# Whole-sequence loads by head pair, merged constants, a catch-up at the end of the first phase, and FFN units paced until the next block, in a chunk-selecting attention followed by a squared-ReLU FFN

## The chip, the cores and the metric

The kernel runs on one core of one Trainium2 chip. The metric is the device time of one execution in microseconds (us), median of the runs. Before the change it was 330.38 us (three runs, 330.23 to 330.52; with a fourth run, 330.43).

The engines are called as the profile calls them: PE multiplies matrices, PEld loads its weights, DVE is the vector engine, ACT the scalar engine, POOL the general engine (here it issues most loads and masks the diagonal), SP issues the other transfers.

## The reference, cut to what matters

Four batches, eight heads, 768 positions, head dimension 64. For each query, the keys' chunks of 32 are ranked by an upper bound from each chunk's smallest and largest key; only the best six causal chunks are attended. The result goes through an FFN of 512 to 2048 to 512.

```
k_min, k_max = k_chunks.min(axis=3), k_chunks.max(axis=3)
ub = sum(maximum(q * k_min, q * k_max), axis=-1)          # one bound per query and chunk
top_chunks = argsort(where(causal, ub, -1e9))[..., -6:]
scores = where(sel & causal_by_position, q @ k.T / 8, -1e9)
attn = softmax(scores) @ v
x = attn.transpose(0, 2, 1, 3).reshape(3072, 512)
out = square(maximum(x @ w_in, 0)) @ w_out
```

## The kernel before

Work is cut into eight phases: each batch has a first-half phase (queries 0 to 383) and a second-half phase (queries 384 to 767). A phase goes through four head pairs. Three kinds of work are interleaved:

- stage A of a pair ("selection"): transpose keys and queries on PE, copy them out of PSUM, reduce them to chunk bounds, rank, and write the rank's mask rows beside the queries;
- stage B of a pair: scores on PE (`ps`), exponentials on ACT (`e`), values on PE (`av`), then Ln, Ln and Exp on ACT for the reciprocal (`rc`), and two products on DVE into `xT`;
- FFN units of the block that was finished last: 16 "up" units (4 matmuls `ph`, a ReLU, a square) and 12 "down" units (4 matmuls `py` each), 28 for each block of 384 tokens. They are put between score matmuls to fill PE while ACT makes exponentials. `run_ffn` is called after each score matmul and decides how many.

```
def run_ffn(cols):                       # before
    pace["due"] += cols * pace["rate"]
    while pace["due"] >= 1.0 and ffn:
        ffn.pop(0)[1]()
        pace["due"] -= 1.0
# ... cut ...
    behind.append(lambda j=j, es=es: values(j, es))     # values lag behind scores
    if len(behind) == HT + LAG:                          # HT = 3, LAG = 2
        for _ in range(HT):
            behind.pop(0)()
# ... cut: for each phase ph ...
    cols = sum(768 if x[2] == 0 else 1920 for x in items if x[0] == "B")
    pace["rate"] = (len(ffn) + nunits - KEEP) / cols if ph else 0.0    # nunits 28, KEEP 8
```

The rate counts the units that are left plus the 28 that the lagging values will release early in the phase, less 8 that are kept for the next phase's start.

The build puts the instructions of each engine into a list order of its own; an instruction with nothing to wait for can come long before its place in the program (the memsets of L410 in the next section, written for the second phase, run from 5.27 us).

The softmax here doesn't subtract the row's maximum and nothing guards it: scores larger than these inputs give would overflow.

## Time and profile before

330.38 us; the profiled run spans 328.7 us. The head of the page: the span, the busy time of each engine with its share, and the busy share of PE, DVE and the granted PE clock in 40 slices of 8.2 us (a digit is tenths).

```profile
span 328.7 us, 6090 instructions
PE 294.6 (90%) x2076; PEld 158.7 (48%) x2096; DVE 219.1 (67%) x678; ACT 218.2 (66%) x540; POOL 99.1 (30%) x237
PE   1397699999998999999999999999999999999995
DVE  7987879778899867999485488994576213421420
PEclk9999999999999999999999999999999999999999
```

PE looks full from the sixth slice on. It is not: matmuls overlap (at 54 us a 384-column matmul has a row of 0.33 us, and the next starts 0.162 us after it), so a "busy" PE has room, and the first slices run at half speed although the clock row shows nines. The timeline of PE shows it (start, length, line, what, idle time before with its releaser):

```profile
37.63 0.82 PE L345 MATMUL av_646<-e,vo 128*128 128x384 bf16 x3 [1.77 <-DVE xT L369]
41.61 0.80 PE L288 MATMUL ph<-xT,w_in_sb 128*128 128x384 bf16 x2 [1.58 <-DVE xT L369]
43.26 1.81 PE L288 MATMUL ph<-xT,w_in_sb 128*128 128x384 bf16 x5
54.21 1.88 PE L288 MATMUL ph<-xT,w_in_sb 128*128 128x384 bf16 x10
```

Five FFN matmuls took 1.81 us at 43 us, ten took 1.88 us at 54 us. The pitches show the two speeds: matmuls of 384 columns that follow each other start 0.32 us apart up to 47 us, 0.162 us after 48.

DVE at the start, from its timeline:

```profile
5.27 0.48 DVE L410 MEMSET vo<- 128x512 bf16 x1
5.85 2.11 DVE L410 MEMSET vo<- 128x512 bf16 x4
7.97 0.72 DVE L201 COPY kqc<-kT 64x384 bf16<-64x384 bf16 x2
```

The memsets belong to the second phase in the program, but run first; the first key copy waits for them until 7.97 us.

The end of the chain that ended last (start, length, what):

```profile
296.55 3.88 PE py L302 x18
300.49 2.97 PE py L302 x13
304.13 10.53 PE ph L288 x60
314.93 10.10 PE py L302 x46
325.06 0.59 ACT ob L307
```

### The profile page before, as it was taken

How to read it: one execution, taken by the hardware profiler on the slowest of the kernel's cores; microseconds unless marked ns; L12 is line 12 of the kernel's file. 1: busy time of each engine (PE TensorE's matmuls, PEld its weight loads, DVE VectorE, ACT ScalarE, POOL GpSimd, SP SyncE). 2: the span in 40 equal slices, each digit the busy share in tenths (PEclk: the TensorE clock that was granted, in tenths of full speed). 3: DMA queues.
4: the chain of work that ended last, by engine and by line, in shares of the span. 5: the costliest groups of instructions: out<-in, count | busy, mean ns of one | idle time of the engine just before them, and what ended most of it. 6: DMA issues, size and time to landing. Idle time of an engine off the chain costs nothing.

```text
span 328.7 us, 6090 instructions
## 1 busy us (share of the span) xinstructions
PE 294.6 (90%) x2076; PEld 158.7 (48%) x2096; DVE 219.1 (67%) x678; ACT 218.2 (66%) x540; POOL 99.1 (30%) x237
## 2 busy tenths in 40 slices
PE   1397699999998999999999999999999999999995
PEld 1143344454454445555455455554555555554542
DVE  7987879778899867999485488994576213421420
ACT  6064556786666559887479766787579679973731
POOL 8886840452410722202142222111122311210000
PEclk9999999999999999999999999999999999999999
DMA  6999999999590891000193010000100000001001
GB/s 45 151 148 195 134 159 210 119 127 98 60 102 3 56 194 40 2 1 3 41 101 52 2 66 32 2 1 3 64 34 0 32 34 32 2 0 64 35 33 64
DMA packets 81371, 20.87 MB, mean 63 GB/s; under 512 B 74836, under 2 KB 77756, under 8 KB 81340
## 3 DMA queue, kind: packets, MB, share of 16 engines
q0 software_dynamic: 77344, 13.63, 53.8%
q1 hardware_dynamic: 3996, 6.85, 5.6%
q8 instruction: 16, 0.26, 0.3%
q14 instruction: 15, 0.12, 0.1%
HBM read 27.26 MB, written 6.29 MB: 102 GB/s over the span
## 4 chain that ended last, share of the span: by engine, by line
PE 55%; DVE 24%; ACT 8%; DMA 6%; issue 3%; POOL 2%; ACTq 0%; DVEq 0%
PE py L302 21%; PE ph L288 13%; PE ps L379 8%; DMA w_out_sb<-in_moe_w_out_dram 6%; DVE kr L206 4%; ACT rc L359 4%; DVE xT L369 3%; DVE qsc L201 3%; ACT e L383 2%; DVE kqc L201 2%; PE sT L249 2%; DVE qsc L254 1%; ACT rc L362 1%; PE kT L194 1%; DVE qp L216 1%
## 5 line engine op out<-in xcount | busy, mean ns | idle before, releaser
L383 ACT ACTIVATE e<-ps 128x384 bf16<-128x384 f32 (+2 forms) x288 | 108.6, 430 | 37.1 <-PE ps L379 34.6
L386 POOL TENSOR_SCALAR_AFFINE_SELECT e<-e 128x128 bf16<-128x128 bf16 x192 | 55.9, 302 | 183.4 <-ACT e L383 181.6
L288 PE MATMUL ph<-xT,w_in_sb 128*128 128x384 bf16 x512 | 105.3, 331 | 4.8 <-ACT ht L293 3.0
L293 ACT ACTIVATE ht<-ph 128x384 bf16<-128x384 f32 x128 | 63.3, 503 | 22.6 <-PE ph L288 17.0
L379 PE MATMUL ps<-qsc,kqc 88*128 88x384 bf16 (+2 forms) x288 | 72.2, 303 | 6.2 <-ACT e L383 2.8
L288 PEld LDWEIGHTS <-w_in_sb 128*128 128x128 bf16 x512 | 48.7, 98 | 38.9 <-issue 13.4
L345 PEld LDWEIGHTS <-vo 128*128 128x128 bf16 x288 | 28.0, 101 | 20.9 <-DVE xT L369 3.2
L379 PEld LDWEIGHTS <-kqc 88*128 88x128 bf16 x288 | 27.2, 100 | 21.9 <-issue 5.7
L307 ACT COPY ob<-py 128x512 f32<-128x512 f32 x24 | 14.2, 590 | 25.7 <-PE py L302 25.5
L206 DVE TENSOR_REDUCE kr<-kT 128x24 bf16<-128x768 bf16 (+1 forms) x40 | 30.3, 793 | 0.3
L201 DVE COPY kqc<-kT 64x768 bf16<-64x768 bf16 (+1 forms) x40 | 18.9, 474 | 16.9 <-PE kT L194 16.3
L254 DVE COPY qsc<-sT 24x640 bf16<-24x640 bf16 (+2 forms) x40 | 16.7, 417 | 7.6 <-PE sT L249 6.8
L201 DVE COPY qsc<-qT 64x768 bf16<-64x768 bf16 (+1 forms) x40 | 18.9, 473 | 1.2 <-PE qT L194 0.6
L194 PE MATMUL kT<-ident,kn 128*64 128x128 bf16 x192 | 11.2, 240 | 8.7 <-POOL ident masks.py:199 4.3
L362 ACT ACTIVATE rc<-rc 128x384 f32<-128x384 f32 x32 | 16.5, 516 | 0.2
L194 PEld LDWEIGHTS <-kn 128*64 128x64 bf16 x192 | 6.8, 116 | 16.3 <-issue 6.5
L194 PE MATMUL qT<-ident,qn 128*64 128x128 bf16 x192 | 11.1, 237 | 1.5 <-DMA qn<-in_q_dram 1.3
L194 PEld LDWEIGHTS <-qn 128*64 128x64 bf16 x192 | 6.7, 114 | 9.6 <-DVE kr L206 4.3
L249 PE MATMUL sT<-ident,selb 128*128 128x128 bf16 x80 | 8.6, 233 | 2.7 <-DVE selb L241 2.4
L229 PE MATMUL ub<-kbd,qp 128*128 128x48 bf16 x80 | 7.7, 190 | 3.4 <-DVE qm L217 2.1
L211 DVE COPY kbd<-kr 64x48 bf16<-64x48 bf16 (+1 forms) x40 | 10.0, 251 | 0.5
L234 DVE TENSOR_TENSOR ubm<-ub,ubmask 128x240 f32<-128x240 f32 (+2 forms) x20 | 7.1, 353 | 4.5 <-PE ub L231 4.3
(648 smaller groups left out, 483.5 us busy)
## 6 DMA issues: line engine op xcount, KB each, us to landing
out_dram<-ob SPq DMA_DIRECT2D x24, 256.0 KB
kn<-in_k_dram POOLq DMA_DIRECT2D x3, 768.0 KB, 9.5
qn<-in_q_dram POOLq DMA_DIRECT2D x3, 768.0 KB, 11.6
vo<-in_v_dram POOLq DMA_DIRECT2D x3, 768.0 KB, 10.2
w_out_sb<-in_moe_w_out_dram POOLq DMA_DIRECT2D x1, 2048.0 KB, 21.0
w_in_sb<-in_moe_w_in_dram POOLq DMA_DIRECT2D x1, 1536.0 KB, 11.7
vo<-in_v_dram POOLq DMA_DIRECT2D x6, 128.0 KB, 7.3
kqc<-kqc SPq DMA_DIRECT2D x15, 36.0 KB
```

The source lines that it names most:

```text
L194: nc.tensor.matmul(pt[D * hh:D * hh + D, 128 * j:128 * (j + 1)], lhsT=nat[nm, b][:, 2 * hp + hh, n0 * HT + j], rhs=ident, is_transpose=Tru ...
L201: nc.vector.tensor_copy(ops[s][hh][0:D, cols], pt[rows])
L206: nc.vector.tensor_reduce(kr[:, mm], pt.rearrange("d (c j) -> d c j", j=CH), axis=AX.X, op=op)
L254: nc.vector.tensor_copy(qs[s][hh][D:KC, 128 * u0:128 * t1], sT[32 * hh:32 * hh + NC, :])
L288: nc.tensor.matmul(ph, lhsT=w_in_sb[:, ki, 128 * f:128 * (f + 1)], rhs=xT[:, ki], start=(ki == 0), stop=(ki == NKI - 1))
L293: nc.scalar.activation(ht, ph, ACT.Relu)
L302: nc.tensor.matmul(py, lhsT=h2[f][:, 128 * t:128 * (t + 1)], rhs=w_out_sb[:, f, :], start=(f == 0), stop=(f == NFI - 1))
L345: nc.tensor.matmul(hold["av"][hh][:, off:], lhsT=vo[b % 2].rearrange("p h n d -> p (h n d)")[:, c0:c0 + 2 * D], rhs=es[hh][:, off:], start ...
L362: nc.scalar.activation(rc, rc, ACT.Exp, scale=-1.0)
L379: nc.tensor.matmul(ps[:, off:], lhsT=kq[s][hh][:, 128 * j:128 * (j + 1)], rhs=qs[s][hh][:, q0 + off:q1], start=True, stop=True)
L383: nc.scalar.activation(e[:, off:], ps[:, off:], ACT.Exp, scale=scale)
L386: nc.gpsimd.affine_select(out=e[:, off:off + 128], in_=e[:, off:off + 128], compare_op=ALU.is_ge, fill=0.0, base=0, channel_multiplier=-1, ...
```

## The change

Its intent: load keys, queries and values by head pair over the whole sequence, so that stage A of any half can start; do the constants in a few large memsets before the first data come; take work off DVE in the first phase; release the first block's FFN units sooner; and spread the FFN units so that they don't run out while the next block's values are pending. The diff, cut to its core:

```
-    load_qk(0, 0, 2, (0,), "k")          # halves of the sequence, one or six heads at a time
-    load_qk(0, 2, H, (0,))
+    load_qk(0, "k"); load_qk(0, "q"); load_qk(1)      # a head pair, whole sequence, 192 KB each
+    load_v(0); load_qk(2); load_v(1); load_qk(3); load_w_in(0, 4); load_v(2); load_v(3)
# ... batch 1 and later: pair by pair instead of 768 KB at a time (cut) ...

-    def set_constants(s): ...            # five small memsets for each of 8 sets; vo[1] in 6 parts
+    nc.vector.memset(kbds, 0.0)          # one tile for all sets
+    nc.vector.memset(selbs[:, :, NT - 1], 0.0)
+    nc.vector.memset(selbs[:, :, 0:NT - 1, :, NC:], 0.0)
+    nc.vector.memset(vo[1]... .bitcast(F32)[:, :, D // 2:], ONES)    # two bf16 ones per word

+                if nm == "q" and first:                  # first halves of batch 0
+                    nc.scalar.copy(ops[s][hh][0:D, cols], pt[rows])
-                for hh in range(2):
-                    nc.vector.tensor_copy(kbd[s][rows, :, hh, 12 * n0:12 * n1], kr[rows])
+                nc.vector.tensor_mul(kbd[s][:, :, :, 12 * n0:12 * n1], kr..., own...)

-    put(0, NP, ("A", 0, (1,), True))
+    put(0, NP, L(catch_up), ("A", 0, (1,), True))        # catch_up empties "behind"

-    KEEP = 8
+    KEEP = (12, 7)      # kept at the end of a second-half phase, of a first-half phase
     def run_ffn(cols):
-        pace["due"] += cols * pace["rate"]
+        late = left.get(pace["tb"], 0) > 0               # the last block's values still pending
+        n = len(ffn) if late else len(ffn) - pace["keep"]
+        over = pace["until"] if late else pace["cols"]
+        if n > 0:
+            pace["due"] += n * min(1.0, cols / max(over, cols))
+        pace["until"] -= cols; pace["cols"] -= cols
```

More of the change, by code (lines that the diff above doesn't have):

```diff
@@ L43 @@
     NEG = -32768.0
+    ONES = 1.0 + 0x3F80 / 2.0 ** 23
     NP = H // 2
@@ L63, with load_qk @@
     nat = {}
-    def load_qk(b, h0, h1, halves=(0, 1), what="kq"):
+    def load_qk(p, what="kq"):
+        b, h = p // NP, 2 * (p % NP)
         for nm, src in (("k", k), ("q", q)):
@@ L72, in load_qk @@
                                      name=nm + "n")
-            j0, j1 = HT * halves[0], HT * (halves[-1] + 1)
-            if j1 - j0 == NT:
-                nc.gpsimd.dma_start(
-                    out=nat[nm, b][:, h0:h1].rearrange("p h j d -> p (h j) d"),
-                    in_=src[b, h0:h1].rearrange("h (j p) d -> p (h j) d",
-                                                p=128))
-                continue
-            if h1 - h0 <= j1 - j0:
-                for h in range(h0, h1):
-                    nc.gpsimd.dma_start(
-                        out=nat[nm, b][:, h, j0:j1],
-                        in_=src[b, h, 128 * j0:128 * j1].rearrange(
-                            "(j p) d -> p j d", p=128))
-                continue
@@ L87, in load_qk @@
-            for j in range(j0, j1):
-                nc.gpsimd.dma_start(
-                    out=nat[nm, b][:, h0:h1, j],
-                    in_=src[b, h0:h1, 128 * j:128 * (j + 1)].rearrange(
-                        "h p d -> p h d"))
+            nc.gpsimd.dma_start(
+                out=nat[nm, b][:, h:h + 2].rearrange("p h j d -> p (h j) d"),
+                in_=src[b, h:h + 2].rearrange("h (j p) d -> p (h j) d", p=128))
     vo = [consts.tile([128, H, NT, 2 * D], BF16, tag=f"vo{s}", name="vo")
@@ L95 @@
           for s in range(2)]
-    def load_v(b, half=None):
-        if half is None:
-            nc.gpsimd.dma_start(
-                out=vo[b % 2][:, :, :, 0:D].rearrange("p h j d -> p (h j) d"),
-                in_=v[b].rearrange("h (j p) d -> p (h j) d", p=128))
-            return
-        for j in range(HT * half, HT * half + HT):
-            nc.gpsimd.dma_start(
-                out=vo[b % 2][:, :, j, 0:D],
-                in_=v[b, :, 128 * j:128 * (j + 1)].rearrange("h p d -> p h d"))
@@ L109, with load_v @@
-    load_qk(0, 0, 2, (0,), "k")
+    def load_v(p):
+        b, h = p // NP, 2 * (p % NP)
+        nc.gpsimd.dma_start(
+            out=vo[b % 2][:, h:h + 2, :, 0:D].rearrange("p h j d -> p (h j) d"),
+            in_=v[b, h:h + 2].rearrange("h (j p) d -> p (h j) d", p=128))
+    load_qk(0, "k")
     ident = consts.tile([128, 128], BF16, tag="ident")
     make_identity(nc, ident)
-    load_qk(0, 0, 2, (0,), "q")
-    load_qk(0, 2, H, (0,))
+    load_qk(0, "q")
+    load_qk(1)
     NSET = 2 * NP
-    kq, qs, kbd, selb = [], [], [], []
@@ L118 @@
-    for s in range(NSET):
-        kq.append([consts.tile([KC, S], BF16, tag=f"kq{s}{hh}", name="kqc")
-                   for hh in range(2)])
-        qs.append([consts.tile([KC, S], BF16, tag=f"qs{s}{hh}", name="qsc")
-                   for hh in range(2)])
-        kbd.append(consts.tile([128, 2, 2, NC], BF16, tag=f"kbd{s}", name="kbd"))
-        selb.append(consts.tile([128, NT, 2, 32], BF16, tag=f"selb{s}",
-                                name="selb"))
-    def set_constants(s):
-        nc.vector.memset(kbd[s], 0.0)
-        for hh in range(2):
-            nc.vector.memset(qs[s][hh][D:KC, 0:128], 0.0)
-        nc.vector.memset(selb[s][:, :, :, NC:], 0.0)
-        nc.vector.memset(selb[s][:, NT - 1], 0.0)
-        for hh in range(2):
-            if (s, hh) == (0, 0):
-                nc.scalar.activation(
-                    kq[0][0][D:KC, :].rearrange("c (a j) -> c a j", j=CH),
-                    ident[0:NC, 0:NC].unsqueeze(2).to_broadcast([NC, NC, CH]),
-                    ACT.Copy, scale=NEG)
-            else:
-                nc.sync.dma_start(out=kq[s][hh][D:KC, :], in_=kq[0][0][D:KC, :])
@@ L142 @@
-    set_constants(0)
-    set_constants(1)
+    kqs = consts.tile([KC, NSET, 2, S], BF16, tag="kqs", name="kqc")
+    qss = consts.tile([KC, NSET, 2, S], BF16, tag="qss", name="qsc")
+    selbs = consts.tile([128, NSET, NT, 2, 32], BF16, tag="selbs", name="selb")
+    kbds = consts.tile([128, NSET, 2, 2, NC], BF16, tag="kbds", name="kbd")
+    kbd = [kbds[:, s] for s in range(NSET)]
+    kq = [[kqs[:, s, hh] for hh in range(2)] for s in range(NSET)]
+    qs = [[qss[:, s, hh] for hh in range(2)] for s in range(NSET)]
@@ new lines, with kq_rows @@
+    selb = [selbs[:, s] for s in range(NSET)]
+    def kq_rows(i):
+        dst = kqs[D:KC, i // 2, i % 2]
+        if i == 0:
+            nc.scalar.activation(
+                dst.rearrange("c (a j) -> c a j", j=CH),
+                ident[0:NC, 0:NC].unsqueeze(2).to_broadcast([NC, NC, CH]),
+                ACT.Copy, scale=NEG)
+        else:
+            nc.sync.dma_start(out=dst, in_=kqs[D:KC, 0, 0])
+    own = consts.tile([128, 2], BF16, tag="own")
+    nc.vector.memset(own, 0.0)
+    for hh in range(2):
+        nc.vector.memset(own[D * hh:D * hh + D, hh:hh + 1], 1.0)
@@ L144 @@
+    nc.vector.memset(kbds, 0.0)
+    nc.vector.memset(selbs[:, :, NT - 1], 0.0)
+    nc.vector.memset(selbs[:, :, 0:NT - 1, :, NC:], 0.0)
+    for s in range(NSET):
+        nc.vector.memset(qss[D:KC, s, :, 0:128], 0.0)
+    nc.vector.memset(vo[1].rearrange("p h j d -> p (h j) d").bitcast(F32)[
+        :, :, D // 2:], ONES)
+    for i in range(2 * NP):
+        kq_rows(i)
     for j in range(2):
@@ L170, in load_w_in @@
             in_=moe_w_in[:, cols].rearrange("(ki p) f -> p ki f", p=128))
-    load_v(0, 0)
+    load_v(0)
+    load_qk(2)
+    load_v(1)
+    load_qk(3)
     load_w_in(0, 4)
+    load_v(2)
+    load_v(3)
     def load_w_out():
@@ L188, in stage_a @@
         m = QB * n1 - u0
-        pool, tag = (psf, "ff") if p < NP and n1 == 1 else (pst, "tp")
+        first = p < NP and n1 == 1
+        pool, tag = (psf, "ff") if first else (pst, "tp")
         for nm in ("k", "q"):
@@ L200, in stage_a @@
                 rows = slice(D * hh, D * hh + D)
-                nc.vector.tensor_copy(ops[s][hh][0:D, cols], pt[rows])
+                if nm == "q" and first:
+                    nc.scalar.copy(ops[s][hh][0:D, cols], pt[rows])
+                else:
+                    nc.vector.tensor_copy(ops[s][hh][0:D, cols], pt[rows])
             if nm == "k":
@@ L208, in stage_a @@
                         axis=AX.X, op=op)
-                for hh in range(2):
-                    rows = slice(D * hh, D * hh + D)
-                    nc.vector.tensor_copy(
-                        kbd[s][rows, :, hh, 12 * n0:12 * n1], kr[rows])
+                nkc = NC // 2 * nt
+                nc.vector.tensor_mul(
+                    kbd[s][:, :, :, 12 * n0:12 * n1],
+                    kr.unsqueeze(2).to_broadcast([128, 2, 2, nkc]),
+                    own.unsqueeze(1).unsqueeze(3).to_broadcast(
+                        [128, 2, 2, nkc]))
                 yield
@@ L258 @@
     xTs = {}
-    nunits = NFI + (QB // 128) * (NFI // 4)
     behind = []
-    KEEP = 8
+    KEEP = (12, 7)
     LAG = 2
@@ L317, in ffn_units @@
         return units
-    pace = {"due": 0.0, "rate": 0.0}
+    pace = {"due": 0.0}
     def run_ffn(cols):
-        pace["due"] += cols * pace["rate"]
+        late = left.get(pace["tb"], 0) > 0
[3 more added lines that the diff above has]
+            pace["due"] += n * min(1.0, cols / max(over, cols))
+        pace["until"] -= cols
+        pace["cols"] -= cols
         while pace["due"] >= 1.0 and ffn:
@@ L408, in put, with catch_up @@
         phases[ph][i:i] = items
+    def catch_up():
+        while behind:
+            behind.pop(0)()
     L = lambda f, *a: ("L", lambda: f(*a))
@@ L412 @@
         put(0, max(hp - 1, 0), ("A", hp, (0,), True))
-    put(0, 1, L(load_qk, 0, 0, H, (1,)), L(load_w_in, 4, NFI))
-    put(0, 2, L(load_v, 0, 1))
-    put(0, NP, ("A", 0, (1,), True))
+    put(0, 2, L(load_w_in, 4, NFI))
+    put(0, NP, L(catch_up), ("A", 0, (1,), True))
+    put(0, NP, L(load_qk, NP), L(load_qk, NP + 1))
     for hp in range(1, NP):
         put(1, 0, ("A", hp, (1,), False))
-    put(1, 0, L(load_qk, 1, 0, H), L(load_w_out), L(load_v, 1))
+    put(1, 0, L(load_w_out))
     for b in range(1, B):
@@ L424 @@
         put(e + 1, 0, ("A", p0 + NP - 1, (0, 1), False))
-        if b + 1 < B:
-            put(e + 1, 1, L(load_qk, b + 1, 0, H))
-            put(e + 1, NP, L(load_v, b + 1))
-    phases[0][1:1] = [L(set_constants, 2), L(set_constants, 3)]
-    for ss in range(NP, NSET):
-        put(1, 1, L(set_constants, ss))
-    for j in range(NT):
-        put(1, j // 2 + 1, L(nc.vector.memset, vo[1][:, :, j, D:], 1.0))
-    for ph, items in enumerate(phases):
-        cols = sum(768 if x[2] == 0 else 1920 for x in items if x[0] == "B")
-        pace["rate"] = (len(ffn) + nunits - KEEP) / cols if ph else 0.0
+    for hp in range(2, NP):
+        put(1, hp - 1, L(load_qk, NP + hp))
+    for hp in range(NP):
+        put(1, hp, L(load_v, NP + hp))
+        for b in range(2, B):
+            put(NBLK * b - 2, hp, L(load_qk, NP * b + hp))
+            put(NBLK * b - 1, hp, L(load_v, NP * b + hp))
+    for i in range(2 * NP, 2 * NSET):
+        put(1, 1, L(kq_rows, i))
+    for ph, items in enumerate(phases):
+        b, blk = divmod(ph, NBLK)
+        pace["tb"] = ph - 1
+        pace["cols"] = NP * (768 if blk == 0 else 1920)
+        pace["until"] = 1408 if blk == 0 else 1536
+        pace["keep"] = KEEP[(blk + 1) % NBLK]
         for x in items:
@@ L448 @@
             ffn.pop(0)[1]()
-    while behind:
-        behind.pop(0)()
+    catch_up()
     while ffn:
```

## The prediction

> **What bounds the kernel.** The page gives PE 90% of 328.7 us, DVE 67%, ACT 66%, but a busy PE hides losses. I charged each matmul of the timeline its warm pitch: 162 ns for 384 columns, 216 ns for 512. All need about 257 us. The missing 72 us:
>
> - first matmul at 4.3 us; 3.6 us of tail after the last;
> - about 38 us between 4 and 48 us. There the timeline starts 384-column matmuls 0.32 us apart, half speed, though the page's granted clock reads full; from 48 us it is 0.162 us. [...]
> - about 28 us of bubbles after 48 us, densest in batch 1 (90 to 140 us), where DVE is 80 to 95% busy.
>
> The head is a DVE chain: the windows table has DVE 85 to 97% busy from 5 to 30 us. 5 us of memsets come first; then memsets of the second value buffer (0.48 us each) run from 5.3 us, so the first key copy, whose transposes ended at 5.2 us, starts at 7.97 us. A head pair of the first phase costs DVE about 6.4 us. The last pair's values wait 1.8 us for xT and end in xT at 41.6 us; only then do FFN matmuls flow.
>
> **What the change does.**
> - Merged memsets: about 4 us by element counts at the traced rate (1 element per ns), done as the first keys land (about 5 us). First copy near 5.5 us: gain 2 to 2.5 us, on the chain.
> - First-phase query copies (2 x 0.35 us per pair) go to ACT, which has room; two block-diagonal copies (2 x 0.34 us) become one multiply, about 0.2 us by estimate. About 4 us over the phase, on the chain.
> - Last pair's values run at once: 2 to 3 us, on the chain.
> - Loads: same bytes, whole sequence first. By the traced 150 to 165 KB/us the fourth pair lands near 16 us, before DVE gets to it. Half of batch 1's keys and queries now precede w_out, which should land near 50 us against 60.1; first needed near 51 us, so it may cost 1 to 2 us.
> - So xT of block 0 is ready at 32 to 34 us, full pitch comes at 39 to 41 us. Gain in the head 8 to 10 us.
> - Pacing: about 33 FFN units run in a first-half block's phase and 23 in a second-half one, against 28 each. By traced durations the second-half phase had about 37 us of PE work, the first-half about 30; now about 34 each. Units no longer run out while the previous block's last values are pending. Gain 4 to 6 of the 28 us.
>
> **Prediction:** 330.4 - 9 - 5, less for new collisions: 315 us, 307 to 323 in 8 of 10. Faster by over 2%: 0.87; within 2%: 0.11; slower: 0.02.
>
> **What would show it:** first key copy near 5.5 us; last xT of block 0 near 33 us; 0.162 us pitch from about 40 us; w_out landing near 50 us, PE wait on it under 2 us; loss after that about 23 us; tail 3.6 us.
>
> **What would make it wrong:** the list order that the build makes, not program order, decides (set-up meant for later ran first before), so memsets or catch-up may land elsewhere; w_out or later key loads late behind one another in the saturated queue; q copies on ACT delaying exps; 12 kept units turning the second-half phase ACT-bound (about 36 us), so that balance gains nothing.

It gave a rule for when full speed comes, which the traces do not show, and put full speed 6.7 us after 41.6 us; the clock record has it at 47.1 us, 5.5 us after, and 3.9 us after PE's matmuls begin to follow each other almost without gaps (43.26 us). The forecast's step from `xT` at 32 to 34 us to full pitch at 39 to 41 us is about those 6.7 us and was the author's estimate. 330.4 less 9 less 5 is 316.4, put down as 315.

The numbers behind three of its phrases: ACT "has room" since it is busy for 10.26 of the 25 us from 5 to 30 us before the change; the one multiply's 0.2 us was an estimate without a source, and the trace of after has 0.21 us (128x48); the queue is "saturated" as the page of before has DMA at 9 from the second to the tenth slice (8 to 82 us).

## More of the kernel before

In stage A, the part that the change touches:

```
for hh in range(2):
    nc.vector.tensor_copy(ops[s][hh][0:D, cols], pt[rows])     # keys or queries out of PSUM
# ... cut: keys only: max and min over chunks into kr, then
for hh in range(2):
    nc.vector.tensor_copy(kbd[s][rows, :, hh, 12 * n0:12 * n1], kr[rows])
# ... cut: queries only
nc.vector.tensor_scalar_max(qp[:, 0:m], pt[:, u0 - QB * n0:], 0.0)
nc.vector.tensor_scalar_min(qm[:, 0:m], pt[:, u0 - QB * n0:], 0.0)
```

The trace's clock record begins at 47.1 us with full speed; before it there is no record, and the page fills the row with nines.

Busy time by engine in the last four attention phases (a first-half and a second-half phase of batch 2, then of batch 3, counted from 0):

```profile
core 0: us, PE busy (x) PEld busy (x) DVE busy (x) ACT busy (x) POOL busy (x), PEclk, DMA share, GB/s
158.70:188.70 30.00, 29.06 (x199) 16.00 (x200) 17.34 (x48) 21.71 (x57) 9.49 (x25) 1.00 0.48 54
188.70:230.70 42.00, 40.28 (x324) 22.30 (x325) 33.20 (x97) 30.98 (x81) 7.38 (x24) 1.00 0.05 20
230.70:260.70 30.00, 29.06 (x199) 15.99 (x200) 17.35 (x48) 21.71 (x57) 7.29 (x24) 1.00 0.07 27
260.70:295.20 34.50, 33.33 (x203) 18.99 (x204) 10.64 (x25) 29.84 (x79) 6.99 (x24) 1.00 0.06 24
```

In the first three of these phases PE sets the length (PE busy 96 to 97%, ACT 72 to 74%); in the last one, which has no selection work left, ACT is busy for 29.84 of 34.50 us.

## The result, and the profile after

The kernel after took 328.40 us (328.30 to 328.73, 4 runs) beside 330.43 us of the kernel before: ratio 0.9941, interval 0.9924 to 0.9958. A ratio here is the mean time of one kernel's fast runs over that of the other's of the same rounds, so it is not quite the ratio of the medians. By the mark of 2% this is "the same". The prediction of 315 us (307 to 323) was wrong: of 14 us, two came.

The page of after, the lines that answer to those of before:

```profile
span 326.6 us, 6096 instructions
PE 296.2 (91%) x2096; PEld 159.0 (49%) x2096; DVE 209.1 (64%) x619; ACT 220.4 (67%) x548; POOL 109.6 (34%) x254
PE   1587699999988999999999999999999999999995
DVE  6865668888899878996755278995855113340420
PEclk9999999999999999999999999999999999999999
```

DVE lost 10 us of work, as planned, and the time hardly noticed. (20 more matmuls of PE are recorded, not made: some records were missing from the trace of before.)

Where did the time go? I cut both traces at the first exponential of chosen phases, and at the last exponential's end. All values in us, from the starts and ends of the exponentials in the trace; the last column is the span.

```
                          head  phase 1  batch 1  batch 2  batch 3   tail    span
before                   45.48    37.14    76.08    71.97    64.55  33.42   328.7
after                    42.61    36.25    73.28    71.81    66.46  36.19   326.6
after less before        -2.87    -0.89    -2.80    -0.16    +1.91  +2.77    -2.0
new pacing alone (d1)    45.48    37.24    71.72    71.80    66.37  36.18   328.8
d1 less before            0.00    +0.10    -4.36    -0.17    +1.82  +2.76    +0.1
```

"Head" is all until the first exponential of phase 1, "tail" all after the last exponential. Up to 224 us the kernel after had earned 6.7 us; then it gave back 4.7 us, 1.9 in the last batch and 2.8 in the tail. Part of the 6.7 is only work put off: at the start of batch 2 the kernel before has run 77 FFN units and the kernel after 72.75 (weight loads in the trace, four to a unit). Four "down" units take about 3.5 us (an estimate from the tail below: 10.36 us for 12), and they are run in the tail. The run with the new pacing alone (below) has the same two losses, so they are the pacing's.

The tail, in the chain that ended last:

```profile
291.04 10.36 PE py L300 x48
302.08 10.53 PE ph L286 x60
312.61 10.38 PE py L300 x48
323.01 0.59 ACT ob L305
```

Before, 6.9 us of kept "down" matmuls stood here ahead of the last block (3.88 and 2.97 us); now 10.36 us, 48 matmuls, 12 units. They run at full speed (one starts 0.216 us after the other, as in the tail of before) and PE waits for nothing there; they are just late. The predicted tail of 3.6 us is the time after the last matmul, and it stayed (before 328.7 less 325.0, after 326.6 less 323.0); that an extra four units would stand before it was overlooked.

The last four attention phases:

```profile
152.10:186.40 34.30, 33.48 (x221) 17.95 (x219) 17.74 (x47) 22.38 (x57) 7.86 (x24) 1.00 0.15 30
186.40:224.00 37.60, 36.09 (x308) 20.44 (x306) 32.64 (x94) 30.53 (x80) 7.64 (x25) 1.00 0.06 22
224.00:258.20 34.20, 33.38 (x220) 17.90 (x219) 17.72 (x47) 22.28 (x57) 6.82 (x23) 1.00 0.06 24
258.20:290.40 32.20, 30.71 (x191) 17.58 (x189) 10.47 (x25) 29.26 (x79) 7.30 (x25) 1.00 0.07 25
```

The phases were balanced as planned: 30.0 and 42.0 us became 34.3 and 37.6. Their sum did not change (72.0, 71.9), because PE sets the length of both (busy 33.48 of 34.30 us and 36.09 of 37.60): a unit moved costs as much there as it saved here. In the last phase, where ACT is busy 29.26 of 32.20 us, taking five units away (27.25 FFN units before, 22.25 after, counted by their weight loads in the trace, four to a unit) shortened it by only 2.3 us, while the phase before grew by 4.2 us.

The start. DVE, from its timeline:

```profile
3.77 1.34 DVE L128 MEMSET vo<- 128x1536 f32 x1 [0.37 <-issue]
6.01 0.72 DVE L198 COPY kqc<-kT 64x384 bf16<-64x384 bf16 x2 [0.90 <-PE kT L188]
12.66 0.29 DVE L215 TENSOR_SCALAR qp<-qT 128x256 bf16<-128x256 bf16 x1 [0.36 <-ACT qsc L196]
17.20 0.29 DVE L215 TENSOR_SCALAR qp<-qT 128x256 bf16<-128x256 bf16 x1 [0.81 <-ACT qsc L196]
22.12 0.29 DVE L215 TENSOR_SCALAR qp<-qT 128x256 bf16<-128x256 bf16 x1 [0.71 <-ACT qsc L196]
```

The constants are done in time: the second value buffer's ones, six memsets of 512 elements before (0.48 us each), are one of 1536 words now (1.34 us). Back-to-back memsets of 128x512 bf16 start 540.7 ns apart in before, those of 24x128 words 140.6 ns apart in after: 1.04 ns per element by the difference. (Their rows in the trace are 485 and 165 ns long.) The first key copy starts at 6.01 us instead of 7.97; what it waits for now is data (the first keys, 192 KB, land at 5.39 us, 4.07 us after their issue began, 1.14 us of it the issue on POOL; two loads of 48 KB landed at 3.92 and 4.85 us before). But DVE then waits for ACT: `qp` reads the same PSUM tile as ACT's two query copies (0.95 us together), and in this trace it starts only when they are done: three waits of 0.36, 0.81 and 0.71 us. The prediction counted no such wait.

And PE at the end of the first phase:

```profile
31.82 0.80 PE L350 MATMUL av_470<-e,vo 128*128 128x384 bf16 x3 [1.09 <-DVE xT L374]
35.54 0.80 PE L350 MATMUL av_494<-e,vo 128*128 128x384 bf16 x3 [1.06 <-DVE xT L374]
39.50 0.80 PE L286 MATMUL ph<-xT,w_in_sb 128*128 128x384 bf16 x2 [1.64 <-DVE xT L374]
41.98 0.85 PE L384 MATMUL ps<-qsc,kqc 88*128 88x384 bf16 x2
```

The last scores of the first phase are exponentiated by 31.1 us, but the first block's `xT` is ready only at 39.4 us (41.6 before, 32 to 34 predicted): each pair's values wait until the products of the pair before free the one pair of value banks, 3.7 us from the third pair's values to the fourth's. In the same stretch the selection for pair 0's second half runs from 28.7 us (transposes) to 41.7 us (mask rows), and the next scores wait for it. DVE even stood idle for 2.6 us at 27.2 us. Full speed comes at 45.7 us instead of 47.1 (39 to 41 predicted); the clock record begins there, and the page's row shows nines before it, though matmuls of 384 columns start 0.32 us apart at 41 us.

### The profile page after: what moved, and what is told of

Read it like the earlier page. It is cut to its first block, busy times and chain, and to the rows that moved or that the text cites. A ratio compares the mean times of both kernels' runs of the same rounds, so it can differ in the third digit from the quotient of the medians.

```text
span 326.6 us, 6096 instructions
## 1 busy us (share of the span) xinstructions
PE 296.2 (91%) x2096; PEld 159.0 (49%) x2096; DVE 209.1 (64%) x619; ACT 220.4 (67%) x548; POOL 109.6 (34%) x254
## 4 chain that ended last, share of the span: by engine, by line
PE 67%; DVE 13%; ACT 11%; issue 4%; POOL 3%; DMA 2%; ACTq 0%; POOLq 0%
PE py L300 22%; PE ph L286 19%; PE ps L384 10%; ACT e L388 4%; ACT rc L364 4%; DVE xT L374 3%; PE kT L188 2%; DVE qsc L198 2%; DMA kn<-in_k_dram 2%; PE sT L248 2%; ACT ht L291 2%; ACT rc L367 2%; DVE kr L203 1%; PE qT L188 1%; PE ub L228 1%
## 5 line engine op out<-in xcount | busy, mean ns | idle before, releaser
L388 ACT ACTIVATE e<-ps 128x384 bf16<-128x384 f32 (+2 forms) x288 | 110.0, 434 | 28.0 <-PE ps L384 24.9
L286 PE MATMUL ph<-xT,w_in_sb 128*128 128x384 bf16 x512 | 109.9, 332 | 6.0 <-ACT ht L291 4.2
L384 PE MATMUL ps<-qsc,kqc 88*128 88x384 bf16 (+2 forms) x288 | 74.3, 304 | 3.8 <-ACT e L388 3.3
L291 ACT ACTIVATE ht<-ph 128x384 bf16<-128x384 f32 x128 | 64.3, 509 | 13.5 <-PE ph L286 11.3
L198 DVE COPY qsc<-qT 64x768 bf16<-64x768 bf16 (+1 forms) x32 | 16.1, 504 | 3.4 <-PE qT L188 3.0
L85 POOL DMA_DIRECT2D vo<-in_v_dram x16 | 16.4, 1036 | 2.5 <-PE ps L384 1.9
L75 POOL DMA_DIRECT2D kn<-in_k_dram x16 | 16.6, 1039 | 1.5 <-POOLq L480 0.8
L75 POOL DMA_DIRECT2D qn<-in_q_dram x16 | 16.4, 1031 | 0.0
L188 PE MATMUL qT<-ident,qn 128*64 128x128 bf16 x192 | 10.3, 237 | 1.5 <-DMA qn<-in_q_dram 1.1
## 6 DMA issues: line engine op xcount, KB each, us to landing
w_in_sb<-in_moe_w_in_dram POOLq DMA_DIRECT2D x1, 1536.0 KB, 11.2
```

The source lines that it names most:

```text
L75: nc.gpsimd.dma_start(out=nat[nm, b][:, h:h + 2].rearrange("p h j d -> p (h j) d"), in_=src[b, h:h + 2].rearrange("h (j p) d -> p (h j) d" ...
L188: nc.tensor.matmul(pt[D * hh:D * hh + D, 128 * j:128 * (j + 1)], lhsT=nat[nm, b][:, 2 * hp + hh, n0 * HT + j], rhs=ident, is_transpose=Tru ...
L286: nc.tensor.matmul(ph, lhsT=w_in_sb[:, ki, 128 * f:128 * (f + 1)], rhs=xT[:, ki], start=(ki == 0), stop=(ki == NKI - 1))
L291: nc.scalar.activation(ht, ph, ACT.Relu)
L384: nc.tensor.matmul(ps[:, off:], lhsT=kq[s][hh][:, 128 * j:128 * (j + 1)], rhs=qs[s][hh][:, q0 + off:q1], start=True, stop=True)
L388: nc.scalar.activation(e[:, off:], ps[:, off:], ACT.Exp, scale=scale)
```

## The experiments

Eighteen kernels; each was correct. Each is compared by its ratio to the kernel before run on the same chip. A difference of 0.01 in a ratio is 3.3 us.

### First call: one part of the change undone

**u1: old pacing put back** (rate and 8 kept, catch-up stays).

```
-    pace["due"] += n * min(1.0, cols / max(over, cols))
+    pace["due"] += cols * pace["rate"]        # and the old rate, KEEP = 8
```

> The kernel after with the old pacing alone put back (constant rate, 8 units kept). Theory A (the new pacing only trades waits of PE on DVE for waits of PE on ACT and is worth nothing): 327.4 to 329.4 us, beside 328.4 of the kernel after. Theory B (the pacing gained the 4 to 6 us that I predicted and some other part lost as much): 332 to 335 us.

Measured: 332.25 us, ratio 1.0060 (1.0045 to 1.0075), 2 us slower than the kernel before. My theory A fell as stated, but B did not follow either, since two parts of the change meet here: with the catch-up, the first block's 28 units are in the list when phase 1's rate is worked out, and the old formula adds another 28. So phase 1 takes 26 units (18 in after, 21.25 before) and has run out of them before its end: from 76 to 88 us PE loads weights for 4 FFN matmuls, 28 in the kernel before. The windows around the end of phase 1:

```profile
74.00:84.10 10.10, 8.80 (x79) 4.65 (x78) 8.80 (x21) 9.74 (x27) 4.31 (x10) 1.00 0.73 72
84.10:87.50 3.40, 3.40 (x22) 1.98 (x18) 2.01 (x13) 1.86 (x5) 1.26 (x4) 0.50 0.06 8
87.50:90.00 2.50, 1.70 (x20) 1.05 (x20) 1.27 (x3) 2.11 (x6) 1.55 (x3) 0.99 0.00 0
```

PE went thin while ACT was 96% busy (9.74 of 10.10 us), and the clock column (after the POOL count) fell to 0.50 for 3.4 us; it did so once more at 121.7 us. Both half-speed stretches are 3.41 us long in the trace's clock record.

**u2: the catch-up taken out** (new pacing stays).

```
-    put(0, NP, L(catch_up), ("A", 0, (1,), True))
+    put(0, NP, ("A", 0, (1,), True))
```

> The kernel after without the catch-up at the end of the first phase. Theory A (the end of the first phase is a serial chain values, Ln, Ln, Exp, two products, next values, through one pair of value banks, and the last values of the chain don't wait for program order): last product of block 0 within 1.5 us of 39.4 us, whole time 328 to 330 us. Theory B (catching up is worth 2 to 3 us on the chain, as predicted): 330.5 to 331.5 us.

Measured: 329.17 us, ratio 0.9955 (0.9936 to 0.9975), beside 0.9941 of after: 0.5 us, within the intervals. The first block's last product ended at 40.7 us instead of 39.4. So the catch-up brings `xT` 1.2 us forward and is worth little in the end.

**u3: the first phase's query copies back on DVE.**

```
-                if nm == "q" and first:
+                if False:
```

> The kernel after with the first phase's query copies back on DVE. Theory A (DVE waits for ACT's copies before it makes qp, so 0.95 us on ACT stand where 0.72 us on DVE stood, and nothing was taken off the chain): 327.4 to 329.2 us. Theory B (3 us of DVE work were taken off the chain, as predicted): 330.5 to 332 us.

Measured: 326.82 us, ratio 0.9889 (0.9864 to 0.9914). That is below both ranges: moving the copies to ACT, meant to gain, cost 1.7 us in the kernel after (0.9941 less 0.9889). The traces do not put this in the head, where DVE waits for ACT: the first exponential of phase 1 comes at 42.86 us in u3 and 42.61 in after. u3 is ahead in phase 1 (34.81 against 36.25 us) and in batch 1 (71.61 against 73.28). PE has full speed from 41.8 us in u3, from 45.7 in after; and the profiled run of u3 (325.45 us) was 1.3 us or more faster than its other three. So u3 gives a cost, and not its cause; n2 below tests the cause.

**u4: the loads of before put back**, with their places.

```
-    load_qk(0, "k"); load_qk(0, "q"); load_qk(1) ...
+    load_qk(0, 0, 2, (0,), "k"); load_qk(0, 0, 2, (0,), "q"); load_qk(0, 2, H, (0,)) ...
```

> The kernel after with the loads before (halves of the sequence first, wider loads) and their places. Theory A (whole-sequence loads deliver the first heads later: first transpose 5.4 us against 4.3, keys of pairs 1 to 3 waited for 0.5 to 0.9 us each): first transpose near 4.4 us, first exponential 1 to 2 us earlier, 326.4 to 328 us. Theory B (the loads cost nothing or gain): 328.4 to 330.5 us.

Measured: 329.21 us, ratio 0.9964 (0.9949 to 0.9979). The first transpose did come earlier (4.34 us), but the first exponential came later (16.2 us against 14.3), so theory A fell; the new loads gain up to 0.8 us, not clear of noise. This too is a sum: up to the first exponential of phase 1 they gain 2.2 us (44.82 us in u4, 42.61 in after), and over phase 1 and batch 1, with the same 69.75 FFN units, they lose 1.6 us (107.98 and 109.53 us). Why they lose it is not shown.

### Second call: parts alone, and the chain at the end of the first phase

**d1: the new pacing alone on the kernel before.** The edit is the pacing part of the diff above.

> The kernel before with the new pacing alone. Theory C (pacing is worth by itself about the 3.9 us by which the kernel after got slower without it): 325.5 to 327.5 us. Theory D (that loss came from the catch-up meeting the old rate, which then counts the first block's 28 units twice in the second phase; pacing by itself is worth at most 1.5 us): 329 to 330.5 us.

Measured: 329.99 us beside 329.97, ratio 1.0002 (0.9987 to 1.0017). As theory D said, the pacing by itself is worth nothing, but the table above shows that this zero is a sum: 4.4 us gained in batch 1, 1.8 lost in batch 3, 2.8 lost in the tail. Most of the gain is work put off: at the start of batch 2 d1 is 4.3 us ahead but has run 73 FFN units, the kernel before 77, and the four missing ones, about 3.5 us by the estimate above, stand in the tail. What is left of the gain is under 1 us. (With the values lagging as before, phase 1 took 20 units, 40 were left for the tail, 36 before.)

**u5: after with the old pacing and without the catch-up.** Both edits of u1 and u2.

> The kernel after with the old pacing and without the catch-up. Theory C: the loss without the pacing stays, 331.5 to 333.5 us. Theory D: it goes with the catch-up, 328.5 to 330.5 us, and the waits of score matmuls on exponentials after 48 us fall from the 13.8 us of the run with old pacing and catch-up to about 9 us.

Measured: 326.26 us, ratio 0.9878 (0.9857 to 0.9899): outside both ranges, on D's side. With u2 this is a clean pair: same kernel, new pacing against old, 0.9955 against 0.9878. The new pacing costs 2.5 us there. Batch 3 and the tail lose more than that, 4.6 us: 64.61 and 33.42 us in u5, 66.46 and 36.19 in u2. Up to batch 3 u2 is only 1.6 us ahead, with about four units fewer done. PE's waits for exponentials before scores (start-to-start distance of matmuls less the full-speed pitch (0.162 us for 384 columns), where the last semaphore came from ACT, summed from 48 to 300 us) were 7.5 us, 10.4 in u2.

**n1: after with the query copies on DVE and no lag of values in the first phase.**

```
-            if len(behind) == HT + LAG:
+            if len(behind) == HT + (LAG if p >= NP or blk else 0):
```

> The kernel after with query copies on DVE and the values of the first phase not lagged at all. If the end of the first phase is bound by the serial chain through the one pair of value banks, starting that chain a head pair earlier brings the last product of block 0 to 34 to 36 us (38.8 with the query copies on DVE alone) and the time to 322 to 325 us. If it is bound by DVE's sum of work or by the order of PE, it stays at 38 to 40 us and the time at 326 to 328 us.

Measured: 325.26 us, ratio 0.9859 (0.9844 to 0.9873); u3, the same with the lag, 0.9889; that is 1.0 us, and the intervals overlap. The last product came at 37.2 us (38.75 in u3), not at 34 to 36. The chain through the value banks is one of the limits, not the only one.

**n2: after with `qp` and `qm` made before ACT's query copies.**

```
+            if nm == "q" and first:
+                qp = work.tile(...); qm = work.tile(...)
+                nc.vector.tensor_scalar_max(qp[:, 0:m], pt[:, u0 - QB * n0:], 0.0)
+                nc.vector.tensor_scalar_min(qm[:, 0:m], pt[:, u0 - QB * n0:], 0.0)
             for hh in range(2):      # the copies follow
```

> The kernel after with qp and qm made before ACT's query copies. If what the move to ACT cost was DVE's wait for ACT before qp, the waits (0.4, 0.8, 0.7 us in the kernel after) are gone and the time is at or under that of the query copies on DVE (326.8): 325 to 327 us. If it was something else (ACT's work before the exponentials), it stays at 328 to 329 us.

Measured: 324.14 us, ratio 0.9823 (0.9806 to 0.9839): 3.9 us faster than after, 2.2 faster than u3, and below the range of 325 to 327 us. Its DVE timeline has no wait for ACT before these instructions:

```profile
7.67 0.28 DVE L196 TENSOR_SCALAR qp<-qT 128x256 bf16<-128x256 bf16 x1
13.02 0.29 DVE L196 TENSOR_SCALAR qp<-qT 128x256 bf16<-128x256 bf16 x1
18.59 0.28 DVE L196 TENSOR_SCALAR qp<-qT 128x256 bf16<-128x256 bf16 x1
```

The first exponential of phase 1 came at 38.6 us (42.6 in after); all later stages are equal to within 0.2 us. That is 4.0 us for 1.9 us of waits; PE also had 6.8 us at full speed from 32.5 us on, which after did not have, and how the rest came about is not shown. So the move to ACT was sound; the order around it was not.

### Third call

**d2: merged constants and the one multiply alone**, on the kernel before.

```
-    set_constants(0); set_constants(1) ...    # and two copies into kbd for each stage A
+    nc.vector.memset(kbds, 0.0) ...           # and one tensor_mul into kbd
```

> The kernel before with the merged constants and the one multiply for the block-diagonal tile alone (old loads, query copies on DVE, old pacing, no catch-up). Theory E (the DVE time that these free early, about 2.5 us before the first key copy and 0.4 us a pair, is on the chain of the first phase): first key copy near 5.8 us against 7.97, last product of block 0 near 38 us, time 326 to 328.5 us. Theory F (the first phase waits for data, so DVE only idles instead): last product of block 0 over 40 us and 329 to 330.5 us.

Measured: 327.42 us, ratio 0.9937 (0.9922 to 0.9952). First key copy at 5.47 us, last product of block 0 at 39.8 us, 1.8 us later than theory E said; the gain lies inside its range. This part alone gives as much as the whole change.

**n3: n2 without the lag in the first phase.** Both edits.

> The kernel after with qp and qm before ACT's query copies, and the first phase's values not lagged at all. If the chain of values and products is what ends last in the first phase, 322 to 323.5 us against 324.1 with qp first alone. If the selection of pair 0's second half (which gates the next scores at 38.6 us there) is, no gain: 323.7 to 325 us.

Measured: 324.45 us, ratio 0.9844 (0.9822 to 0.9866): no gain on n2.

**n4: n2 with pair 0's second-half selection beside the last scores of the first phase.**

```
-    put(0, NP, L(catch_up), ("A", 0, (1,), True))
+    put(0, NP - 1, ("A", 0, (1,), False))
+    put(0, NP, L(catch_up))
```

> As the run with qp first, and the selection of pair 0's second half is put beside the last pair's scores of the first phase instead of after them (its keys and queries are there from about 7 us with whole-sequence loads). If that selection, a chain of about 12 us through DVE and one PSUM bank, is what empties PE between 31 and 40 us: first exponential of the second phase at 33 to 36 us instead of 38.6, 320 to 322.5 us. If DVE's sum of work or the values chain is the limit: within 1 us of 324.1.

Measured: 324.27 us, ratio 0.9839 (0.9822 to 0.9855); first exponential of phase 1 at 38.2 us, 38.6 in n2. No gain. In n1 to n4 PE reached full speed near 29 to 33 us for 3.4 to 6.8 us, fell back to half, and came to full speed for good only at 42 to 43 us (mean granted clock of the four profiled runs 0.984 to 0.995).

**n6: n2 with the old pacing and no catch-up.**

> The run with qp first with the old pacing and no catch-up. Theory G (the new pacing leaves the second-half phases with too few FFN units, so that scores wait on exponentials: 10.4 us against 7.5 with the old pacing, and it costs 2 to 3 us whatever the head does): 321 to 323 us. Theory H (the 2.9 us between the two runs without catch-up were chance of the build's order): 323.5 to 326 us.

Measured: 322.47 us, ratio 0.9791 (0.9775 to 0.9808), as theory G said. Against n2, the last batch and the tail are 4.6 us shorter together (64.63 and 33.42 us; 66.43 and 36.18 in n2), batch 1 is 2.8 us longer.

### Fourth call: is it the number of units kept back?

**k1: u2 with 8 and 8 kept**, **k2: u2 with 16 and 3 kept**; and **k3: u5 with 7 kept instead of 8**, to see how far the time moves with the build's order alone.

```
-    KEEP = (12, 7)
+    KEEP = (8, 8)          # k1;  (16, 3) in k2
-    KEEP = 8
+    KEEP = 7               # k3, old pacing
```

> The kernel after without catch-up, new pacing, but 8 and 8 units kept instead of 12 and 7. If the units kept back starve the second-half phases, most of the 2.9 us come back: 326 to 327.3 us, waits of scores on exponentials after 48 us near 8 us (10.4 with 12 and 7). If it is the spreading until the last block is done, 328.5 to 329.5 us.

> The same with 16 and 3 kept. If the units kept back starve the second-half phases: slower than 12 and 7 (329.2), 330.5 to 333 us, waits of scores on exponentials over 11 us. If they don't matter: 328.5 to 329.5 us.

> The kernel after without catch-up and with the old pacing, 7 units kept instead of 8: a change that every theory gives no weight, to see how far the time moves with the build's order alone. Within 0.7 us of 326.3 if differences of 2 us between these kernels can be read; 1.5 us or more off it if they can't.

Measured: k1 325.83 us, ratio 0.9856 (0.9825 to 0.9887); u2 0.9955; k2 330.25 us, 1.0007 (0.9985 to 1.0030). k3 326.72 us, 0.9889 (0.9873 to 0.9905), 0.4 us from u5, so steps of 3 to 5 us are unlikely to be the build's chance (this is one such test). k1 and k2 came out 0.2 us below their ranges. By stage, from the exponentials as above, with the FFN units left for the tail:

```
                     batch 1  batch 2  batch 3   tail   units in the tail
k1  (8, 8)             75.98    71.57    64.89  33.20        36
u2  (12, 7)            74.94    70.95    66.46  36.19        40
k2  (16, 3)            69.39    71.52    69.74  38.75        43.25
u5  old pacing, 8      76.74    72.01    64.61  33.42        36
```

What is kept back for the next phase's start shortens batch 1 and costs more in batch 3 and the tail. The shorter batch 1 is largely work put off again: at its end k1 and u5 have run 77 units, u2 73 and k2 69. The waits of PE for exponentials before scores (48 to 300 us, as above) were 6.9, 10.4 and 11.2 us. So the units kept back are the cause, not the spreading. Both numbers of the pair were changed together, so which of the two costs more is open. The last two attention phases of k1 (compare those of after: 34.20 and 32.20 us):

```profile
226.50:257.20 30.70, 29.89 (x204) 16.29 (x203) 17.45 (x46) 21.63 (x56) 7.07 (x24) 1.00 0.07 27
257.20:291.40 34.20, 32.99 (x203) 18.85 (x202) 10.80 (x26) 29.88 (x79) 6.97 (x25) 1.00 0.06 24
```

**n7: n6 with the early second-half selection of n4.**

> The kernel after with the old pacing, no catch-up, qp and qm before ACT's query copies, and the selection of pair 0's second half beside the last pair's scores. Beside 322.5 us without the last of these: 321.5 to 323 us, as the same move gained nothing with the new pacing (324.3 against 324.1).

Measured: 322.21 us, ratio 0.9767 (0.9749 to 0.9786), 2.3% faster than before and the only kernel here with its whole interval beyond 2%; n6 had 0.9791, so the early selection's share is not clear of noise.

### Fifth call

**d3: d1 with 8 and 8 kept.**

> The kernel before with the new pacing alone and 8 and 8 kept. If the units kept back (12 and 7) ate what the spreading gains, this is faster than with 12 and 7 (330.0): 326.5 to 328.7 us, waits of scores on exponentials after 48 us near 8 us instead of 10.5. If the 8 and 8 only suits the other parts of the change: 329.5 to 330.5 us.

Measured: 328.91 us, the median of the three fast runs, ratio 0.9973 (0.9946 to 1.0001); one run of 732 us, which the profile happened to take, is set aside as slow, so there is no stage table and no wait to read. Between the two expectations: not settled on the kernel before.

**n8: n7 with the new pacing, 8 and 8 kept.**

> As n7 but with the new pacing, 8 and 8 kept. Beside 322.2 us: 321 to 322.5 us, since 8 and 8 measured 325.8 where the old pacing measured 326.3.

Measured: 322.29 us, ratio 0.9765 (0.9729 to 0.9800), equal to n7. With a small number kept, the new pacing is as good as the old, not better.

## Why the prediction was wrong

**The pacing** ("Gain 4 to 6 of the 28 us") is the step that failed most: with the other parts it cost 2.5 us (u2 against u5), alone it gave 0 (d1). In d1 batch 1 became 4.4 us shorter, but about 3.5 us up to there are the four units put off, which come back as 2.8 us of tail; the spreading itself gained under 1 us, and batch 3 lost 1.8 us. Two errors. First, the balance argument contradicted itself: 37 and 30 us of PE work became "about 34 each", which is the same sum, and where PE sets the length of both phases a moved unit gains nothing (batch 2: 72.0 and 71.8 us). Second, the end was left out: units kept back at the end of the last phase are no reserve but 2.8 us of plain tail, and pay only where the earlier phases become shorter by more. "12 kept units turning the second-half phase ACT-bound" stood among the things that could go wrong; the last phase (29.26 of 32.20 us of ACT) fits it; the second-half phase of batch 2 does not (PE 36.09 of 37.60 us). k1, u2 and k2 tie the loss to the number kept.

**The head** ("xT of block 0 is ready at 32 to 34 us ... Gain in the head 8 to 10 us") came to 2.9 us. The step that failed is that the head is one DVE chain, so that DVE time saved comes off it one for one. That held for the start (7.97 to 6.01 us; d2 is worth 2.1 us), and then no longer: after 27 us DVE idles, and the end of the phase is a chain of round trips. Term by term:

- Merged constants, predicted 2 to 2.5 us with the multiply's share on top: 2.1 us for both (d2). Right in kind; the first copy came at 6.01 us instead of 5.5 because the larger first load lands later (d2, with the old loads, has 5.47 us).
- Query copies on ACT, predicted to be most of "4 us over the phase": minus 1.7 us (u3). DVE waited for ACT on the shared PSUM tile. With the order turned the kernel is 3.9 us faster (n2 against after), and the copies gain 2.2 us on u3. That the waits are what u3 won back is not shown, since u3's head is no shorter.
- Last pair's values at once, predicted 2 to 3 us: 0.5 us (u2), not clear of noise.
- Loads: w_out landed at 51.8 us (predicted 50) and PE never waited for it, right; the fourth pair's keys and queries landed at 17.6 and 19.1 us instead of 16. The loads are worth up to 0.8 us (u4): 2.2 gained in the head, 1.6 lost by the end of batch 1.

The four steps on the way from before to after, by ratios: constants and multiply -2.1 us (d2), loads and query copies -1.9 (u5 less d2), new pacing +2.5 (u2 less u5), catch-up -0.5 (after less u2); together -2.0 us. The parts are not additive: the query copies cost 1.7 us in the kernel after, while with the loads they gained in u5; the build's order differs in each, and I have no run that explains that difference.

What stays open is the end of the first phase. Freeing the values from their lag brought `xT` 1.5 us forward in n1 and nothing forward in n3; starting the second-half selection sooner (n4) brought `xT` 0.8 and the next scores 0.4 us forward. The time hardly moved, while PE fell back to half speed for 3.4 to 10.2 us between 33 and 43 us. Neither chain alone is the limit; whether they and the half speed hold each other up was not shown.

## What to carry to other kernels

When filler work is moved between stages, add up the stages that the same engine bounds: here the sum didn't change (72.0 and 71.8 us in batch 2), and what was still in reserve at the end was tail (2.8 us). When work is moved to a second engine, look for what else reads the same PSUM tile: here the other reader waited (0.36 to 0.81 us a time), and with the reader on the chain first the kernel was 3.9 us faster (n2). A part that measures zero can be a gain and a loss; cut the trace into stages before dropping it, count the work done by the end of each stage (work put off looks like a gain), and try the number that causes the loss.
